# Conditioned adaLN block with memory attention on one core: a new prologue order, constants on VectorE, Wo and a memory update at other places, split last tiles

## The chip, the cores and the metric

The kernel runs on 1 core of one Trainium2 chip. A core has TensorE (PE, matrix products; its weight loads are listed as PEld), VectorE (DVE), ScalarE (ACT), GpSimd (POOL) and SyncE (SP). Here SP does nothing but issue DMAs; ACT issues some as well. Each engine works through its own instructions in order and waits for semaphores of the others. PE writes its products into PSUM, in buffers that DVE or ACT must read before they can be used again.

The metric is device time in microseconds (us) of one execution, as the median of several runs. Before the change it is 259.25 us (11 runs, 257.18 to 260.23).

## The reference

One transformer block on `x` of 2048 rows by 448, bf16, with 16 heads of 28. Cut to what matters:

```python
mod = (_silu(c) @ w_mod).reshape(c.shape[0], 6, 1, -1)          # six vectors of 448
sa, ca, ga, sb, cb, gb = ...
h = _layernorm(x) * (1 + ca) + sa
x = x + ga * _A_ref(h, A_wq, A_wk, A_wv, A_wo, A_beta)
h = _layernorm(x) * (1 + cb) + sb
x = x + gb * _B_ref(h, B_w_gate, B_w_up, B_w_down)

# _A_ref: 4 segments of 512 rows; per segment and head
p = _softmax(qs @ ks.T * scale + mask)          # causal inside the segment
a_dot = p @ vs
a_mem = (phi(qs) @ M) / (phi(qs) @ z + 1e-6)    # phi(t) = t + 1 if t > 0 else exp(t)
o = g * a_mem + (1 - g) * a_dot                 # g = sigmoid(beta)
M = M + phi(ks).T @ vs ;  z = z + sum(phi(ks))
# all heads together, then @ wo

# _B_ref: h = sigmoid(x @ w_gate) * (x @ w_up); h @ w_down      (448 -> 1792 -> 448)
```

## The kernel before, in words

The 2048 rows are four segments (`s`) of 512, each of four row tiles (`t`) of 128. The 448 columns are four chunks (`k` or `kc`), three of 128 and one of 64 (`LW`). The 16 heads are four groups (`hc`) of four. A pair (s, hc) is a unit of attention.

**An order written by hand.** The kernel is built under a manual schedule: the order in which Python emits instructions is their order on each engine. The main loop runs over `s`, `hc` and three logit groups `g` (0, 1, 2). In each step it emits the logits of the group (`logits`, L402), whose exponentials are ACT's, then for the unit before (`prev`) the memory read (`mem_read`, L457, at g = 0), the products with the values (`pv`, L429, at g = 1) and the transposing DMA of the result (`otr`, L482, at g = 2). The rest of PE's work is in a queue of jobs, `fill`, each with a cost in planned nanoseconds; `run_fill` (L584) takes as many as `pace` allows per step. Small work of DVE, POOL and SP is put off with `later(ns, ...)` (L76) until a planned clock, moved on by `tick` (L88), has passed; `need` (L92) forces what isn't due yet.

**Prologue (L639 to L679).** 18 products into an unused PSUM tile (`warm_up`). Norm of segment 0 (`LN`, L256). `mod_cols` (L212) makes columns of the modulation vectors by products with one moving column: (0, 0) gives `sa`, from `wm[0]`, which SP loads; (1, 1) gives `1 + ca`, from `wm[1]`, which ACT's queue loads; `mod_evac` (L230) copies them out of PSUM on DVE. 16 transposes on PE bring the normed tiles to column layout. `1 + ca` is folded into the rows of wq, wk (`pad_copy`, L618, on DVE, which also spreads heads from 28 to 32 columns) and wv (POOL, L673); `sa` becomes one more row of each (`bias_rows`, L627: products of a column of `sa` with wq, wk or wv; then a copy of the row into the weight). wq and wk first land in a staging part of `wd_sb`.

**Stages.** While the units of segment s are attended, `fill` works off the projections of later segments (`proj_qk` L335, `proj_v` L347), the memory updates (`mem_k` L373 makes phi of the keys and transposes it by DMA, `mem_update` L381 does the products `dM` and adds them to `M_sb`), and, from s = 1 on, what belongs to segment s - 1: four tiles of Wo (`wo_tile`, L492, with the second norm's statistics), gate and up (`gate_up` L514, `gate_up2` L533, a group of two chunks of 128 out of 14) and later down (`down`, L543, 14 products a tile, an add on DVE, the store). After the loop the last segment's Wo, gate, up and down follow.

**Queues and buffers.** All transposing DMAs (`pk`, `hT`, `oT`) and all stores of the output are issued by SP in the order of emission. PSUM has one tile `lg` of four banks for logits, and four buffers that everything else (pq, pv, acc, mem, dM, pwo, gps, ups, dps) shares in turn: the n-th allocation waits until the (n - 4)-th has been read. `acc` and `mem` are read by three DVE instructions, the last of which (L452 or L449, and L471) frees the buffer.

`KEEP` says how many gate and up groups a segment leaves for the next, `EARLY` is the first segment's pace, `NWARM` the number of warm-up products. `MM`, `MV`, `TR` and `GU` are the planner's costs of a product of 512 columns, of 448, of a transpose, and of a gate and up group.

Of the kernel before, what the change touches and what calls it, by code (L numbers as in the profile page):

```python
# [13 lines left out]
P = 128  # L14
# [3 lines left out]
def kernel(  # L18
# [34 lines left out]
    NWARM, EARLY, KEEP = 18, 2400.0, (0, 2, 2, 4)  # L53
# [111 lines left out]
    nc.gpsimd.memset(wo_sb[:], 0.0)  # L165
# [10 lines left out]
    for b in ou_bufs:  # L176
        nc.vector.memset(b[:, :, :, Dh:HP], 0.0)
    coef = const.tile([P, 2, H], F32)
# [10 lines left out]
    vt_all = [const.tile([P, TPS, H, ME + 1], BF16, name=f"vt{s}") for s in range(NSEG)]  # L189
    silu_bc = const.tile([KP, NK, P], BF16)  # L190

    def late_consts():
        nc.vector.tensor_copy(silu_bc[:], silu[:].rearrange("p (k o) -> p k o", o=1).to_broadcast([KP, NK, P]))
        for s in range(NSEG):
            nc.gpsimd.memset(vt_all[s][:, :, :, Dh:Dh + 1], 1.0)
# [5 lines left out]

        nc.gpsimd.memset(bmask[:], 1.0)
        for hs in range(4):
            nc.gpsimd.affine_select(out=bmask[:, :, hs, :], in_=bmask[:, :, hs, :], compare_op=ALU.is_ge,
                                    fill=0.0, base=-HP * hs, pattern=[[0, NHC], [0, ME]], channel_multiplier=1)
            nc.gpsimd.affine_select(out=bmask[:, :, hs, :], in_=bmask[:, :, hs, :], compare_op=ALU.is_ge,
                                    fill=0.0, base=HP * hs + Dh - 1, pattern=[[0, NHC], [0, ME]],
                                    channel_multiplier=-1)
# [220 lines left out]
    def pv(s, hc):  # L429
# [21 lines left out]
        t1 = work.tile([P, TPS * 4, Dh], F32, tag="t1", bufs=1)  # L451
# [5 lines left out]
    def mem_read(s, hc):  # L457
# [11 lines left out]
        t2 = work.tile([P, TPS * 4, Dh], F32, tag="t2", bufs=2)  # L469
# [21 lines left out]

    def wo_tile(s, t):  # L492
        need("wo")
        pw = m_f32("pwo")
        for k in range(NK):
            nc.tensor.matmul(pw[:, 0:D], lhsT=oT_of[s][:, k, t, :], rhs=wo_sb[:, k, :],  # L496
                             start=(k == 0), stop=(k == NK - 1))
# [7 lines left out]
        later(1500, lambda: ln.norm_t(t), ("ln2", s))  # L505
# [37 lines left out]
    def down(s, t):  # L543
        need("wd")
        dp = m_f32("dps")
        for fc in range(NFC):
            nc.tensor.matmul(dp[:, 0:D], lhsT=fT_of[(s, fc)][:, t * P:(t + 1) * P], rhs=wd_sb[:, fc, :],  # L547
                             start=(fc == 0), stop=(fc == NFC - 1))
        ot = work.tile([P, D], BF16, tag="ot", bufs=2)
        i = s * TPS + t  # L550
        nc.vector.tensor_tensor(ot[:], dp[:, 0:D], x_sb[:, i, :], ALU.add)  # L551
        nc.sync.dma_start(out_dram[i * P:(i + 1) * P, :], ot[:])


# [262 lines left out]
```

The softmax here doesn't subtract the row's maximum and nothing guards it: scores larger than these inputs give would overflow.

## Time and profile before

| | |
|---|---|
| median of 11 runs | 259.25 us (257.18 to 260.23) |
| the profiled execution: time | 259.45 us |
| its span, first to last instruction | 257.7 us |
| mean granted TensorE clock | 0.993 |
| HBM read, written | 10.67 MB, 1.84 MB |

The profile is of one execution. Its page counts, for each engine, the time in which it executes something; waiting, branches and the issuing of DMAs don't count. A line of the page names the code line, engine, operation and the tiles written and read; "idle before" is how long the engine had stood still, and what it stood for. The costliest groups:

```profile
L418 ACT ACTIVATE pT<-lg 128x2048 bf16<-128x2048 f32 (+1 forms) x48 | 76.8, 1599 | 27.3 <-PE lg L415 26.9
L426 POOL TENSOR_SCALAR_AFFINE_SELECT pT<-pT 128x512 bf16<-128x512 bf16 x64 | 42.8, 685 | 58.9 <-ACT pT L418 58.9
...
L541 DVE SCALAR_TENSOR_TENSOR fT<-tt,ups 128x512 bf16<-128x512 f32 x56 | 37.0, 685 | 32.9 <-PE ups L538 30.4
L547 PE MATMUL dps<-wd_sb,fT 128*128 128x448 bf16 x224 | 43.9, 352 | 0.0
L521 PE MATMUL gps<-hT,wg_sb 128*128 128x512 bf16 x154 | 40.3, 379 | 1.8 <-DVE t L452 1.0
```

After the bar stand the group's busy time and the mean length of one instruction in ns, then the idle time. Products on PE overlap: one of 512 columns is listed with some 380 ns, but they follow each other every 0.22 us in an undisturbed stretch. The chain of work that ended last, traced back from the end, is PE for 73% of the span and DVE for 13%.

### The profile page before, as it was taken

Reading aid. Unit: us, or ns where it says so; the run is one execution under the profiler, and the core shown is the slowest. Engines: PE = TensorE matmul, PEld = TensorE weight load, DVE = VectorE, ACT = ScalarE, POOL = GpSimd, SP = SyncE. Lnnn points to the kernel's source line nnn. Section 1 sums busy time; section 2 is a strip of 40 time slices with the busy share of each in tenths; the row PEclk is TensorE's granted clock in tenths of the full one; section 3 lists DMA queues with packets and bytes.
Section 4 is the critical chain, followed back from the end, with each engine's and each line's share of the span. In section 5 each row is a group of like instructions: output and inputs, shape, how many; then the busy total and the mean of one; then the engine's idle time right before and its main releaser. Section 6 shows DMA issues by size and latency. Waiting matters only on the chain.

```text
span 257.7 us, 5277 instructions
## 1 busy us (share of the span) xinstructions
PE 241.5 (94%) x2037; PEld 113.2 (44%) x2062; DVE 175.2 (68%) x412; ACT 139.1 (54%) x173; POOL 79.3 (31%) x146
## 2 busy tenths in 40 slices
PE   7799997999988899999999999999999999999994
PEld 2434533455544344544544534454344445333352
DVE  4878898577996768988965667886565485644411
ACT  1369878499859597876427767353653300133300
POOL 3388355141547221362602123352030023000000
PEclk9999999799999999999999999999999999999999
DMA  5999998577123103211221110123210013200011
GB/s 150 268 251 253 353 269 138 84 166 104 43 43 62 23 0 68 56 23 20 61 64 34 20 23 1 22 43 78 56 22 3 0 20 81 74 0 0 3 36 36
DMA packets 40992, 19.66 MB, mean 76 GB/s; under 512 B 29704, under 2 KB 40072, under 8 KB 40968
## 3 DMA queue, kind: packets, MB, share of 16 engines
q1 hardware_dynamic: 39544, 18.53, 32.1%
q10 hardware_dynamic: 1424, 0.80, 1.3%
q8 instruction: 16, 0.26, 0.5%
q14 instruction: 8, 0.07, 0.1%
HBM read 10.67 MB, written 1.84 MB: 49 GB/s over the span
## 4 chain that ended last, share of the span: by engine, by line
PE 73%; DVE 13%; DMA 5%; ACT 4%; issue 4%; POOL 1%; DVEq 0%; ACTq 0%
PE dps L547 17%; PE ups L538 12%; PE gps L521 12%; PE pq L340 8%; PE acc L440 5%; PE gps L526 5%; PE pwo L496 5%; PE lg L415 4%; DVE st L266 3%; DMA hT<-xn 2%; ACT pT L418 2%; DMA x_sb<-in_A_x_dram 2%; DVE xn L274 2%; PE pv L352 1%; PE dM L388 1%
## 5 line engine op out<-in xcount | busy, mean ns | idle before, releaser
L418 ACT ACTIVATE pT<-lg 128x2048 bf16<-128x2048 f32 (+1 forms) x48 | 76.8, 1599 | 27.3 <-PE lg L415 26.9
L426 POOL TENSOR_SCALAR_AFFINE_SELECT pT<-pT 128x512 bf16<-128x512 bf16 x64 | 42.8, 685 | 58.9 <-ACT pT L418 58.9
L529 ACT ACTIVATE tt<-gps 128x512 f32<-128x512 f32 x56 | 30.4, 596 | 56.1 <-PE gps L526 56.1
L541 DVE SCALAR_TENSOR_TENSOR fT<-tt,ups 128x512 bf16<-128x512 f32 x56 | 37.0, 685 | 32.9 <-PE ups L538 30.4
L547 PE MATMUL dps<-wd_sb,fT 128*128 128x448 bf16 x224 | 43.9, 352 | 0.0
L521 PE MATMUL gps<-hT,wg_sb 128*128 128x512 bf16 x154 | 40.3, 379 | 1.8 <-DVE t L452 1.0
L538 PE MATMUL ups<-hT,wu_sb 128*128 128x512 bf16 x165 | 40.6, 381 | 0.3 <-issue 0.2
L547 PEld LDWEIGHTS <-fT 128*128 128x128 bf16 x224 | 21.5, 98 | 19.9 <-issue 0.2
L270 POOL TENSOR_SCALAR rs<-mv 128x1 f32<-128x1 f32 (+2 forms) x21 | 5.9, 283 | 61.4 <-DVE mv L267 58.6
L521 PEld LDWEIGHTS <-wg_sb 128*128 128x128 bf16 x168 | 15.8, 98 | 19.6 <-DVE t L452 1.6
L538 PEld LDWEIGHTS <-wu_sb 128*128 128x128 bf16 x168 | 14.1, 97 | 20.9 <-issue 6.8
L266 DVE BATCH_NORM_STATS2 st<-x_sb 128x6 f32<-128x448 bf16 x32 | 19.8, 619 | 2.5 <-DMA x_sb<-in_A_x_dram 2.0
L440 PE MATMUL acc<-vt,pT 128*128 128x29 bf16 x640 | 18.7, 175 | 1.5 <-DVE t L471 1.0
L440 PEld LDWEIGHTS <-pT 128*128 128x128 bf16 x640 | 17.6, 96 | 4.8 <-issue 2.1
L340 PE MATMUL pq<-hT,wq_sb 128*128 128x512 bf16 x58 | 16.4, 381 | 2.5 <-DMA hT<-xn 2.3
L340 PE MATMUL pq<-hT,wk_sb 128*128 128x512 bf16 x62 | 17.4, 396 | 1.2 <-DVE t L452 1.1
L551 DVE TENSOR_TENSOR ot<-dps,x_sb 128x448 bf16<-128x448 f32 x16 | 9.9, 621 | 12.5 <-PE dps L547 9.4
L526 PE MATMUL ups<-hT,wgu_sb 64*128 64x512 bf16 x56 | 17.7, 382 | 0.5 <-DVE t L452 0.5
L415 PE MATMUL lg<-qT,kT 28*128 28x512 bf16 (+3 forms) x256 | 17.5, 305 | 0.5 <-ACT pT L418 0.5
L274 DVE TENSOR_SCALAR xn<-x_sb,mv,rs 128x448 bf16<-128x448 bf16 x32 | 14.1, 457 | 5.6 <-POOL rs L271 5.6
L526 PE MATMUL gps<-hT,wgu_sb 64*128 64x512 bf16 x56 | 16.9, 381 | 0.1
L271 POOL TENSOR_TENSOR rs<-rs,mhalf 128x1 f32<-128x1 f32 (+2 forms) x21 | 13.8, 656 | 1.8
(101 smaller groups left out, 262.1 us busy)
## 6 DMA issues: line engine op xcount, KB each, us to landing
wm<-in_w_mod_dram SPq DMA_DIRECT2D x5, 392.0 KB, 6.3
out_dram<-ot SPq DMA_DIRECT2D x16, 112.0 KB, 1.7
x_sb<-in_A_x_dram SPq DMA_DIRECT2D x3, 448.0 KB, 4.7
wd_sb<-in_B_w_down_dram SPq DMA_DIRECT2D x3, 448.0 KB, 9.9
wg_sb<-in_B_w_gate_dram SPq DMA_DIRECT2D x3, 448.0 KB, 9.8
wu_sb<-in_B_w_up_dram SPq DMA_DIRECT2D x3, 448.0 KB, 10.2
wm<-in_w_mod_dram ACTq DMA_DIRECT2D x1, 392.0 KB
wo_sb<-in_A_wo_dram SPq DMA_DIRECT2D x4, 98.0 KB
```

What stands on the lines that cost most here:

```text
L266: nc.vector.bn_stats(st[:], self.srcs[i])
L340: nc.tensor.matmul(pq[:, 0:L], lhsT=head_cols(w_sb, k, hc), rhs=h[:, k, :], start=(k == 0), stop=(k == NK - 1))
L415: nc.tensor.matmul(lg[:, hs, wid:wid + nq], lhsT=kT[r, hc, kb * P:(kb + 1) * P], rhs=qT[r, hc, kb * P:L], start=True, stop=True, tile_posi ...
L418: nc.scalar.activation(pT[:, :, w0:w0 + wid], lg[:, :, 0:wid], AF.Exp, scale=scale)
L426: nc.gpsimd.affine_select(out=blk, in_=blk, compare_op=ALU.is_ge, fill=0.0, base=0, pattern=[[0, 4], [1, P]], channel_multiplier=-1)
L440: nc.tensor.matmul(accv[:, qb, hs, 0:ME], lhsT=pT[:, hs, c0:c0 + P], rhs=vt[:, kb, hc * 4 + hs, 0:ME], start=(kb == 0), stop=(kb == qb))
L521: nc.tensor.matmul(g[:, 0:L], lhsT=wg_sb[:, k, f], rhs=h[:, k, :], start=(k == 0), stop=False)
L526: nc.tensor.matmul(dst[:, 0:L], lhsT=wgu_sb[r:r + LW, f], rhs=h[r:r + LW, 3, :], start=first, stop=not first, tile_position=(r, 0))
L529: nc.scalar.activation(tt[:], g[:, 0:L], AF.Tanh, scale=0.5)
L538: nc.tensor.matmul(u[:, 0:L], lhsT=wu_sb[:, k, f], rhs=h[:, k, :], start=False, stop=(k == 2))
L541: nc.vector.scalar_tensor_tensor(ft[:], tt[:], 1.0, u[:, 0:L], op0=ALU.add, op1=ALU.mult)
L547: nc.tensor.matmul(dp[:, 0:D], lhsT=fT_of[(s, fc)][:, t * P:(t + 1) * P], rhs=wd_sb[:, fc, :], start=(fc == 0), stop=(fc == NFC - 1))
```

## The change

- **Prologue.** `NWARM` is 20, and a product without use stands after each group of four transposes and after the bias rows. `mod_cols(((1, 1),))` comes first, `mod_cols(((0, 0),))` after half of the transposes; `mod_evac` and the norms change places to suit. The bias rows of wq and wk are made together, that of wv later and alone; the first two projections follow each other.
- **Constants.** The fills of `wo_sb`, of `bmask` and of the ones in `vt` go from POOL to DVE, to the start; the eight selects that shape `bmask` stay on POOL, and go to the start too.
- **Segment 2's norm** (`ln1_start(2)`) is started ahead of segment 1's transposes.
- **Wo one group sooner.** The jobs of segment s - 1 are put into `fill` at (hc 0, g 2) instead of (hc 1, g 0), with jobs of the old tail between the Wo tiles in another pattern; there the transposing DMA `otr` is emitted ahead of the fill work. The second norm's scaling is put off by 2400 planned ns instead of 1500, but for the last segment.
- **The third memory update** (`m[2]`) goes from the loop of s = 1 to that of s = 2.
- **t1 and t2**, the attention's two summands, become bf16.
- **The end.** `KEEP` is 3 for the last segment, the pace there divides by 10; a number of jobs (`run_jobs`) replaces planned time around the last unit; the first two Wo tiles do their first three chunks ahead of the last chunk's wait. Stores of segments 2 and 3 go out by ACT's queue. The last tile of all is done in two halves of 224 columns.

```diff
-    NWARM, EARLY, KEEP = 18, 2400.0, (0, 2, 2, 4)
+    NWARM, EARLY, KEEP = 20, 2400.0, (0, 2, 2, 3)
...
-    nc.gpsimd.memset(wo_sb[:], 0.0)
...
+    nc.vector.memset(bmask[:], 1.0)
+    for hs in range(4):
+        nc.gpsimd.affine_select(out=bmask[:, :, hs, :], ...)
+        nc.gpsimd.affine_select(out=bmask[:, :, hs, :], ...)
+    nc.vector.memset(wo_sb[:], 0.0)
+    for vt in vt_all:
+        nc.vector.memset(vt[:, :, :, Dh:Dh + 1], 1.0)
...
     def late_consts():
-        for s in range(NSEG):
-            nc.gpsimd.memset(vt_all[s][:, :, :, Dh:Dh + 1], 1.0)
...
-        nc.gpsimd.memset(bmask[:], 1.0)
-        for hs in range(4):
-            nc.gpsimd.affine_select(...)
...
-        t1 = work.tile([P, TPS * 4, Dh], F32, tag="t1", bufs=1)
+        t1 = work.tile([P, TPS * 4, Dh], BF16, tag="t1", bufs=1)
...
-        t2 = work.tile([P, TPS * 4, Dh], F32, tag="t2", bufs=2)
+        t2 = work.tile([P, TPS * 4, Dh], BF16, tag="t2", bufs=2)
...
+    def wo_mm(s, t, ks):
+        need("wo")
+        if t not in pw_of:
+            pw_of[t] = m_f32("pwo")
+        for k in ks:
+            nc.tensor.matmul(pw_of[t][:, 0:D], lhsT=oT_of[s][:, k, t, :], rhs=wo_sb[:, k, :],
+                             start=(k == 0), stop=(k == NK - 1))
     def wo_tile(s, t):
+        wo_mm(s, t, range(NK))
+        wo_fin(s, t)
...
-        later(1500, lambda: ln.norm_t(t), ("ln2", s))
+        later(1500 if s == NSEG - 1 else 2400, lambda: ln.norm_t(t), ("ln2", s))
...
     def down(s, t):
...
+        eng = nc.scalar if s >= NSEG - 2 else nc.sync
+        n = 2 if i == NSEG * TPS - 1 else 1
+        for h in range(n):
+            c = slice(h * D // n, (h + 1) * D // n)
+            for fc in range(NFC):
+                nc.tensor.matmul(dp[:, c], lhsT=fT_of[(s, fc)][:, t * P:(t + 1) * P], rhs=wd_sb[:, fc, c], ...)
+            nc.vector.tensor_tensor(ot[:, c], dp[:, c], x_sb[:, i, c], ALU.add)
+            eng.dma_start(out_dram[i * P:(i + 1) * P, c], ot[:, c])
...
-        return [(0, lambda: [later(2000 * hc, ...
+        return [(0, lambda: [later((2000 if s < 2 else 1500) * hc, ...
...
+    def run_jobs(n):
+        for _ in range(n):
+            cst, fn = fill.popleft()
+            fn()
+            tick(cst)
...
-    mod_cols(((0, 0),), warm[:, 1, :])
-    for t in range(TPS):
+    mod_cols(((1, 1),), warm[:, 2, :])
+    for t in range(2):
         ln0.norm(t)
-    mod_evac(((0, 0),))
+    mod_evac(((1, 1),))
+    for t in range(2, TPS):
+        ln0.norm(t)
     pts = [m_bf16("lntr") for _ in range(NK)]
-    for t in range(TPS):
+    def ln0_tr(t):
         for kc in range(NK):
             nc.tensor.transpose(pts[kc][:, t * P:(t + 1) * P], ln0.xn[:, t, kc * P:(kc + 1) * P], ident[:])
-    mod_cols(((1, 1),), warm[:, 2, :])
+        warm_up(1)
+    ln0_tr(0)
+    ln0_tr(1)
+    mod_cols(((0, 0),), warm[:, 1, :])
+    mod_evac(((0, 0),))
+    for k in range(2):
+        pad_copy(nc.vector, wq_sb, wq_st, k)
+    ln0_tr(2)
+    ln0_tr(3)
     for kc in range(NK):
         ln0.pe_evac(pts[kc], kc, True)
-    mod_evac(((1, 1),))
-    evac_q, = bias_rows((wq_st,))
-    for k in range(NK):
-        pad_copy(nc.vector, wq_sb, wq_st, k)
+        if kc == 1:
+            pad_copy(nc.vector, wq_sb, wq_st, 2)
+    evac_q, evac_k = bias_rows((wq_st, wk_st))
+    pad_copy(nc.vector, wq_sb, wq_st, 3)
+    warm_up(1)
     evac_q(nc.scalar.copy, wq_sb[LW:LW + 1, 3, :, 0:Dh])
     for k in range(NK):
         pad_copy(nc.vector, wk_sb, wk_st, k)
+    evac_k(nc.vector.tensor_copy, wk_sb[LW:LW + 1, 3, :, 0:Dh])
...
     j0[0][1]()
-    evac_k, evac_v = bias_rows((wk_st, wv_sb))
-    evac_k(nc.vector.tensor_copy, wk_sb[LW:LW + 1, 3, :, 0:Dh])
+    j0[1][1]()
+    evac_v, = bias_rows((wv_sb,))
...
-    ... + j0[11:] + ln1_pe_jobs(1) + [ln1_start(2)] + j1[:4] ...
+    ... + j0[11:] + [ln1_start(2)] + ln1_pe_jobs(1) + j1[:4] ...
...
+                if prev[0] >= 0 and g == 2 and hc == 0:
+                    otr(*prev)
-                if s >= 1 and hc == 1 and g == 0:
+                if s >= 1 and hc == 0 and g == 2:
...
-                    for w in wo_jobs(s - 1):
+                    for t, w in enumerate(wo_jobs(s - 1)):
+                        n = 2 if s > 1 or t == 0 else t % 2
+                        fill.extend(tail[:n])
+                        tail = tail[n:]
                         fill.append(w)
-                        if tail and s > 1:
-                            fill.extend(tail[:2])
-                            tail = tail[2:]
...
                         dj = down_jobs(s - 2)
+                        if s == 2:
+                            gj = m[2][0:1] + gj[:6] + m[2][1:] + gj[6:]
...
-                        fill.extend(h2_jobs(s - 1) + gj[:2] + m[2][0:1] + gj[2:10] + m[2][1:] + gj[10:])
-                    pace[0] = (cost(fill) - KEEP[s] * GU) / (12 if s < 3 else 9)
+                        fill.extend(h2_jobs(s - 1) + gj)
+                    pace[0] = (cost(fill) - KEEP[s] * GU) / (12 if s < 3 else 10)
...
-                if prev[0] >= 0 and g == 2:
+                if g == 2 and hc > 0:
                     otr(*prev)
...
-    run_fill(2000)
+    run_jobs(4)
     pv(last, NHC - 1)
     tick(1100)
-    run_fill(1500)
+    run_jobs(1)
     otr(last, NHC - 1)
-    run_fill(3500)
-    for c, fn in wo_jobs(last):
-        fn()
-        tick(c)
-    fill.extend(dj)
+    run_jobs(1)
+    for t in range(2):
+        wo_mm(last, t, range(NK - 1))
+    tick(6 * MV)
+    for t in range(TPS):
+        wo_mm(last, t, range(NK - 1 if t < 2 else 0, NK))
+        wo_fin(last, t)
+        tick((200, 1400, 760, 760)[t])
+    fill.extendleft(reversed(dj))
```

## The prediction

> **What bounds the kernel now.** First the page's busy shares and the granted clock, then the engine windows, then the list of what TensorE waited for, then the timeline around the largest waits, last DMA landings.
>
> ```profile
> PE 241.5 (94%) x2037; PEld 113.2 (44%) x2062; DVE 175.2 (68%) x412; ACT 139.1 (54%) x173; POOL 79.3 (31%) x146
> ...
> PEclk9999999799999999999999999999999999999999
> ```
>
> TensorE (PE) is busy 94% of 257.7 us and the change takes no product away, so a gain must come from the other 16 us or from clock. Of those, 1.4 us lie before the first instruction of PE and about 3.3 us behind its last (the last down product starts at 254.06). The clock row has one dent, the 7 in its eighth slice (45 to 51.5 us).
>
> ```profile
> 43.50:45.60 2.10, 0.00 (x0) 0.00 (x0) 2.03 (x6) 1.19 (x2) 2.05 (x4) 1.00 0.50 70
> 46.40:49.90 3.50, 3.50 (x20) 1.48 (x19) 1.75 (x3) 1.30 (x2) 0.00 (x0) 0.51 0.63 80
> ```
>
> Windows, with PE first and the granted clock third from the end: PE stands still for 2.1 us, and 0.8 us later its clock is 0.51 for 3.5 us. That idle time is paid twice: its own length, and 3.5 x 0.49 = 1.7 us.
>
> ```profile
> PE pq L340 <- DMA hT<-xn: 2.3, 1, 2.3
> ...
> PE pq L340 <- DVE t L452: 1.1, 1, 1.1
> PE acc L440 <- DVE t L471: 1.0, 1, 1.0
> PE gps L521 <- DVE t L452: 1.0, 1, 1.0
> PE warm L225 <- DVE silu L187: 0.9, 1, 0.9
> PE pv L352 <- DVE kT L345: 0.6, 1, 0.6
> PE ups L526 <- DVE t L452: 0.5, 1, 0.5
> ```
>
> Waits of PE (total, times, longest). The first is that still-stand: segment 2's first projection waits for its transposed activations. L452, L471 and L345 are VectorE (DVE) instructions that free a PSUM buffer: DVE, far from busy on average, is 7.3 to 7.6 of 8 us busy at 32 to 40 and 64 to 80 us, and late there.
>
> **The prologue: a loss.** `mod_cols(((1, 1),))` now stands ahead of `mod_cols(((0, 0),))` and of every transpose in PE's order. It reads wm1, loaded on ACT's queue.
>
> ```profile
> 1.80 0.49 ACTq L117 DMA_DIRECT2D wm<-in_w_mod_dram  x1
> ...
> 9.84 0.47 SPq L137 DMA_DIRECT2D wv_sb<-in_A_wv_dram  x1
> ...
> 10.29 0.54 PE L225 MATMUL warm<-silu,wm 112*128 112x1 bf16 x16
> ```
>
> The loads of wm land 6.3 to 9.8 us after issue, median 8.0; SP's L137 waited 2.1 us for a wm load and went out at 9.84, which with 1.80 + 8.0 = 9.8 puts wm1's landing there. Before, PE came to it at 10.29 and did not notice. Now PE ends 20 fillers at 7.4 + 2 x 0.22 = 7.8 and stands until 9.85. Then: wm1's 16 columns end at 10.4 (0.54); `cols` on DVE at 10.7, and norms 2 and 3 queue behind it to 11.4 (2 x 0.36; before 10.0). Two transposed tiles with fillers 4 x 0.23 to 11.3, wm0's columns to 11.85, two more tiles and fillers to 12.75. DVE meanwhile: sa_bf 12.2, two wq pads 12.7 (0.27 each), hT 13.1, pad 13.4, hT 13.75, pad 14.0, four wk pads 15.1 (1.07), wk's bias row 15.75 (0.62). The key projection closes at 16.0 (before 15.1). The bias row of wv, four products that shared kv slots before, now stands alone behind it (0.19 each by the starts of L632: 0.8), then the second query projection (0.9): first logits at 17.7 against 16.08, **+1.6**. Bounds: 0, if wm1 flew like wm0 (issued at 1.31, PE's wait for it over at 7.40: 6.1 us, so landing at 7.9), and +1.6; I take the latter, being the landing seen. Five more fillers inside this stretch lie in DVE's shadow and cost nothing of their own; 0.22 each if they did not.
>
> The moved constants hide: DVE idles 2.0 us before the first L266 at 5.08, and the added memsets come to 0.25 + 0.9 + 4 x 0.1 = 1.55 (by the 256-word 0.27 and 128-word 0.17). GpSimd (POOL) gets eight mask selects of 0.33, from 3.5 to 6.2, ahead of its rs at 6.75. Cover gone, each delays the norms one for one. POOL's scaling of wv (5.56 us, L673) starts behind wv's bias row, now at 16.2 instead of 13.6, and ends at 21.8; the first value projection, 21.17 before, comes at 22.8: 1.0 of slack, beyond which PE waits.
>
> **20 to 46 us: a gain.**
>
> ```profile
> 21.55 1.23 POOL L195 MEMSET vt<- 128x64 bf16 x4
> 21.57 1.62 DVE L197 TENSOR_SCALAR coef<-coef 128x16 f32<-128x16 f32 x1 [1.11 <-ACT coef L196]
> ...
> 22.35 0.80 POOL L202 MEMSET bmask<- 128x464 bf16 x1
> ...
> 23.22 0.17 DVE L198 TENSOR_SCALAR coef<-coef 128x16 f32<-128x16 f32 x1
> ```
>
> A 16-column DVE operation takes 1.62 us, as long as POOL's memsets beside it; the like-sized L198 takes 0.17. The memsets leave, so 1.45 comes back. The norms of segment 1 then end at about 26.2 (before 26.0, now with the prologue's +1.6 inside), but PE, later too, no longer waits for them: transposes 26.5 to 27.4 instead of 24.9 to 26.75, and the first projection closes at 28.5 against 28.0. So 1.1 of the 1.6 is recovered.
>
> Segment 2's stats now start one group earlier; from the last hT copy to its last norm DVE has 10.7 us of work (five L266/L267 pairs of 0.77, three kT of 0.68, three phi of 0.75, one ou of 1.1, four norms of 0.37) instead of 12.3 (seven pairs), so that norm ends at 39.0, not 40.15. On SP two of its four transposes (1.2 us issue each) go out ahead of the third pk instead of behind. The last is issued at 40.5, not 41.66, and lands 3.1 later at 43.6. PE arrives at 43.2 to 43.7 (before 43.24; +0.5, less some of the 0.6 at L345). Projection starts at 43.7 against 45.67: **-2.0**, the prologue's loss included. Bounds: -3.3 (no loss there) and +1.6 (no recovery). With 0.5 us or less idle the clock should stay: **-1.7**, between -1.75 and 0.
>
> The Trainium skill ("TensorE: Matmul & The Clock Gate", Why this matters for your kernels) asks only that PE not idle longer than about 3 us between bursts; here 2.1 to 2.4 us sufficed, so the trace decides. The same page (Part 4) says transposes do not count as activity for the clock. That speaks against the new prologue, which from 7.8 to 12.7 holds little but transposes and one-column products; by that rule I should add another 1.7 there, while the row shows 1.00 from 8.4 to 11.2 through the like work.
>
> **70 to 98 us: a gain.** From the memory read of unit (1,0) to the key projection that needs `acc`'s buffer, PE has 6.5 us of work (3 Wo tiles, logits, acc, Wo, dM, pq). DVE has 1.1 + 6.5 = 7.6, hence the wait of 1.1. Wo is queued one group sooner, behind two jobs of the old tail, and the transpose of the last unit goes out on SP ahead of that fill work, so oT is there no later. The new order puts dM after the first Wo tile, delays the norms (2400 planner ns for 1500) and puts the unit's t1 ahead of the third Wo tile: 1.1 + 5.9 = 7.0, wait 0.5. Next, `acc` of (1,1) waited 1.0 for L471; in the new allocation order it takes a buffer that ScalarE frees. Third, L521 waited 1.0 for an L452 queued behind L288, which stood for a DMA; t1 now precedes L288. Fourth, 0.5 at L526: segment 2's `phi` work is gone from here. Of 3.6 I take **-2.6**; bounds -3.6 and 0.
>
> The third memory update reappears in the next segment: DVE 4 x 0.7 + 0.63 = 3.4 us, ScalarE 4 x 0.63, dM 0.84 on PE unchanged, four pk transposes on SP of 1.2 each ahead of the next oT. Windows there show DVE at 4.9 to 7.4 of 8. Nothing to +3.4; with all other new waits I take **+1.0**. bf16 t1/t2: L452 and L471 read PSUM at 0.62 still; L453 gains at most 0.3, off PE's path except at the end.
>
> **200 us to the end.** Before, the last `acc` stood 0.5 for ScalarE (L529) since all four buffers were out; it now follows the up half. From its end the chain to the last oT is 1.1 + 0.3 to 0.6 + 2.45 DMA = 4.2 us; PE's cover is one gate/up group (3.2, from L521 to L521 in the last stage) + six Wo products 1.1 = 4.3. The stalls of 0.5 (L440) and 0.5 (L496) go: **-1.0**, 0 if DVE is late again. Out stores of the last two segments leave SP, so segment 3's last transpose is not behind a store (SP 217.30, then 217.92): PE's stutter at 220.8 to 221.7, **-0.4**, bounds 0 and -0.6. ScalarE then waits for `ot`, with its tanh queued behind; it idles 16.6 us there, so nothing. The halved last tile: DVE 0.62 to about 0.34, **-0.3**; bounds -0.5 (some of the store's 1.7 to landing too) and +0.5 (a second issue on ScalarE's queue, 0.5 by its L117). The Trainium skill ("DMA: Bandwidth & Descriptors", Specifications) names 512 B as the least for line rate, and the halved rows are 448 B; no run here prices it.
>
> **Sum** on the profiled execution (259.45, span 257.7, so 1.75 around it): -2.0 -1.7 -2.6 +1.0 -1.0 -0.4 -0.3 = -7.0; span 250.7, time **252.5**. The median of 11 runs is 259.25, 0.2 below the profiled one; they spread from 257.18 to 260.23.
>
> **Rivals.** (a) Slower: wm1's wait sets off the clock. PE idles 2.0 us from 7.8, much as at 43.5; half clock follows over the projections (+1.7), hT of segment 2 moves with everything (+1.6), PE still idles there and the second dent stays, and DVE's waits merely shift: 259.45 + 3.3 = 262.7. It decides if idle before segment 2 remains at 2 us or more. For it: the single dent followed such an idle; against: DVE's shortened list. (b) DVE remains the limit at 70 to 98 (it was 7.35 of 8 busy): -2.6 becomes 0, 255.1. (c) wm1 lands by 8.4: another 1 to 1.6 off, and the waits at their better bounds, 250. (d) The fillers and moves only exchange waits: 259.
>
> **Chances.** Forecast 0.45, (c) 0.17, (b) 0.20, (d) 0.08, (a) 0.10. About 0.5% (1.3 us) is what a measurement of this kernel can tell from no change. Faster: 0.45 + 0.17 + 0.20 = 0.82; same 0.08; slower 0.10. The range runs from 249.5 (all but the best of (c)) to 256.5 (b with 1.4 of further waits), leaving (a) and (d) out.
>
> **What would show it.** In the new profile: PE's L225 waiting some 2 us for a wm load, first L415 near 17.7; no DVE operation of 1.6 us on `coef`; under 1 us at the first L340 of segment 2 and no dent in the clock row behind it; L452 and L471 gone from the top waits; no 0.5 at the last L440. I am wrong if wm1 is there in time, if the dent stays, or if segment 2 shows new waits above 1 us each.

## The result and the profile after

The change makes the kernel slower: 261.14 us (12 runs, 259.93 to 261.9) against 258.83 us (46 runs, 257.18 to 260.29), a ratio of 1.009 with a 95% interval of 1.0065 to 1.0116. The forecast was 252.5, range 249.5 to 256.5. The profiled execution after took 260.25 us with a span of 258.5, before 259.45 and 257.7.

Two rows of the page after, busy share of TensorE and granted clock by slice:

```profile
PE 241.0 (93%) x2057; PEld 114.8 (44%) x2083; DVE 173.1 (67%) x419; ACT 139.5 (54%) x173; POOL 75.7 (29%) x140
PEclk9999999999999999999999999999999999999999
```

PE's busy time hardly moved (241.5 before), and this execution has no half-clock slice. The waits of PE after (total, times, longest):

```profile
PE warm L225 <- DMA wm<-in_w_mod_dram: 1.6, 1, 1.6
...
PE gps L531 <- DVE hT L288: 1.3, 1, 1.3
PE pq L340 <- DVE ou L449: 1.2, 1, 1.2
PE ups L536 <- DVE t L452: 1.1, 1, 1.1
...
PE dM L388 <- DMA pk<-e: 0.8, 1, 0.8
PE pv L352 <- DVE t L471: 0.7, 1, 0.7
PE ups L536 <- DVE t L471: 0.6, 1, 0.6
PE gps L531 <- DVE t L452: 0.6, 1, 0.6
...
PE dps L563 <- DVE ot L565: 0.5, 1, 0.5
```

Gone are the 2.3 us for hT at segment 2's first projection, the 1.1 and the 1.0 at a projection and an `acc` in the loop of s = 1 (75 and 81.5 us), the 0.5 at the last `acc` and the 0.9 at the first columns. New are the wait for wm1, a wait of the same first projection for another operation (L449), a group at L531/L536 and dM, and one inside the split tile. Where they stand shows when the two profiles are laid side by side by the starts of the same exponential (L418) of each unit, after minus before ("this stretch" is the growth since the row above; that of the second row counts from the start, as its forecast does):

| stretch, up to | difference there | this stretch | forecast |
|---|---|---|---|
| first logits | +2.0 | | (+1.6) |
| segment 2's first projection, 45.69 against 45.67 us | 0.0 | 0.0 | -2.0 |
| (0, 3, 1), behind the half-clock window of before | -1.5 | -1.5 | -1.7 |
| (2, 0, 0), 98.6 us | -2.9 | -1.4 | -2.6 |
| (3, 0, 2), 155.6 us | +2.1 | +5.0 | +1.0 |
| end of the span | +0.8 | -1.3 | -1.7 |

So 5.0 us are lost in the loop of s = 2, and the start of the forecast's gains, segment 2's projection, did not move at all. What VectorE did in the worst stretch, first before the change, then after it (timeline: start, length, what; in brackets its idle time before and for what):

```profile
126.00 0.29 DVE L366 TENSOR_SCALAR r<-qT 128x512 bf16<-128x512 bf16 x1
...
128.72 0.61 DVE L453 TENSOR_TENSOR ou<-t,t 128x448 bf16<-128x448 f32 x1
130.28 1.38 DVE L288 TENSOR_SCALAR hT<-hT,cols 128x512 bf16<-128x512 bf16 x4 [0.94 <-issue]
```

```profile
121.84 1.19 DVE L274 TENSOR_SCALAR xn<-x_sb,mv,rs 128x448 bf16<-128x448 bf16 x2
...
123.98 0.61 DVE L565 TENSOR_TENSOR ot<-dps,x_sb 128x448 bf16<-128x448 f32 x1
128.94 0.74 DVE L288 TENSOR_SCALAR hT<-hT,cols 128x512 bf16<-128x512 bf16 x2 [4.35 <-DMA hT<-xn]
129.59 0.29 DVE L366 TENSOR_SCALAR r<-qT 128x512 bf16<-128x512 bf16 x1
129.99 0.43 DVE L367 TENSOR_TENSOR e<-e,r 128x512 bf16<-128x512 bf16 x1
```

Before, the phi of the next memory read (L366) and a unit's sums (up to L453) stood ahead of the scaling of hT (L288). Now VectorE stands 4.35 us at that scaling, whose last row tile was normed at 123, and behind it wait the phi and the two units' `t`, which free PE's buffers. PE's timeline after:

```profile
130.47 0.39 PE L464 MATMUL mem<-rm,e 128*128 128x116 bf16 x4 [0.34 <-DVE e L367]
131.50 0.81 PE L531 MATMUL gps<-hT,wg_sb 128*128 128x512 bf16 x2 [0.64 <-DVE t L452]
132.67 0.81 PE L531 MATMUL gps<-hT,wg_sb 128*128 128x512 bf16 x3 [0.37 <-DVE ot L565]
...
134.68 0.39 PE L536 MATMUL ups<-hT,wgu_sb 64*128 64x512 bf16 x1 [0.64 <-DVE t L471]
...
140.69 0.39 PE L536 MATMUL ups<-hT,wgu_sb 64*128 64x512 bf16 x1 [1.06 <-DVE t L452]
...
147.87 0.38 PE L388 MATMUL dM<-vt,pk 128*128 128x116 bf16 x4 [0.77 <-DMA pk<-e]
```

The listed lengths of products overlap, so a bracket is some 0.17 us less than what PE lost by the starts (one product of 512 columns follows another in 0.22 us). By the starts PE lost 0.51, 0.81, 0.53 and 0.81 between 129.7 and 134.7, then 1.22 at 139 and 0.93 at 147 round the moved memory update: 4.8 of the 5.0 us. Before there were no waits above 0.5 between 97 and 200 us. Below, a wait of PE in a fence is the profile's, one in the text mostly counted by the starts.

A reading aid for the experiments: of 93 runs of the kernel before that stood beside them, 34 had the full clock (median 257.66) and 59 mostly one half-clock window of 3.4 us (259.39), after the change 5 of 12 (260.25) and 7 (261.36), so it is slower in both groups.

### The profile page after: what moved, and what is told of

Same layout as the page of the kernel before. It is cut to its first block, busy times and chain, and to the rows that moved or that the text cites. A ratio compares the mean times of both kernels' runs of the same rounds, so it can differ in the third digit from the quotient of the medians.

```text
span 258.5 us, 5310 instructions
## 1 busy us (share of the span) xinstructions
PE 241.0 (93%) x2057; PEld 114.8 (44%) x2083; DVE 173.1 (67%) x419; ACT 139.5 (54%) x173; POOL 75.7 (29%) x140
## 4 chain that ended last, share of the span: by engine, by line
PE 56%; DVE 5%; DMA 3%; ACT 3%; issue 2%; POOL 1%; SPq 0%; DVEq 0%
PE dps L563 14%; PE gps L531 13%; PE ups L548 13%; PE gps L536 5%; PE pwo L499 4%; PE acc L440 3%; PE lg L415 3%; DMA hT<-xn 2%; ACT pT L418 2%; DMA pk<-e 1%; PE mem L464 1%; ACT tt L539 1%; DVE e L367 1%; DVE ot L565 1%; POOL pT L426 1%
## 5 line engine op out<-in xcount | busy, mean ns | idle before, releaser
L418 ACT ACTIVATE pT<-lg 128x2048 bf16<-128x2048 f32 (+1 forms) x48 | 76.7, 1598 | 28.3 <-PE lg L415 28.1
L551 DVE SCALAR_TENSOR_TENSOR fT<-tt,ups 128x512 bf16<-128x512 f32 x56 | 37.2, 687 | 40.9 <-PE ups L548 36.5
L563 PE MATMUL dps<-wd_sb,fT 128*128 128x448 bf16 (+1 forms) x238 | 44.1, 342 | 0.5 <-DVE ot L565 0.5
L531 PE MATMUL gps<-hT,wg_sb 128*128 128x512 bf16 x156 | 40.1, 379 | 3.1 <-DVE hT L288 1.3
L563 PEld LDWEIGHTS <-fT 128*128 128x128 bf16 x238 | 22.8, 98 | 19.2 <-issue 0.6
L531 PEld LDWEIGHTS <-wg_sb 128*128 128x128 bf16 x168 | 15.6, 98 | 20.3 <-issue 2.0
L440 PEld LDWEIGHTS <-pT 128*128 128x128 bf16 x640 | 17.5, 96 | 3.3 <-issue 1.5
L536 PE MATMUL ups<-hT,wgu_sb 64*128 64x512 bf16 x56 | 17.4, 382 | 1.7 <-DVE t L452 1.1
L440 PE MATMUL acc<-vt,pT 128*128 128x29 bf16 x640 | 18.6, 175 | 0.0
L270 POOL TENSOR_SCALAR rs<-mv 128x1 f32<-128x1 f32 (+2 forms) x21 | 5.4, 256 | 43.9 <-DVE mv L267 40.9
L536 PE MATMUL gps<-hT,wgu_sb 64*128 64x512 bf16 x56 | 16.9, 381 | 0.2
L565 DVE TENSOR_TENSOR ot<-dps,x_sb 128x448 bf16<-128x448 f32 (+1 forms) x17 | 10.1, 593 | 10.0 <-PE dps L563 10.0
L340 PE MATMUL pq<-hT,wk_sb 128*128 128x512 bf16 x62 | 16.4, 380 | 0.2
L352 PE MATMUL pv<-wv_sb,hT 128*128 128x448 bf16 x64 | 13.4, 353 | 1.3 <-DVE t L471 0.7
```

Source lines behind the costliest of these rows:

```text
L340: nc.tensor.matmul(pq[:, 0:L], lhsT=head_cols(w_sb, k, hc), rhs=h[:, k, :], start=(k == 0), stop=(k == NK - 1))
L418: nc.scalar.activation(pT[:, :, w0:w0 + wid], lg[:, :, 0:wid], AF.Exp, scale=scale)
L440: nc.tensor.matmul(accv[:, qb, hs, 0:ME], lhsT=pT[:, hs, c0:c0 + P], rhs=vt[:, kb, hc * 4 + hs, 0:ME], start=(kb == 0), stop=(kb == qb))
L531: nc.tensor.matmul(g[:, 0:L], lhsT=wg_sb[:, k, f], rhs=h[:, k, :], start=(k == 0), stop=False)
L536: nc.tensor.matmul(dst[:, 0:L], lhsT=wgu_sb[r:r + LW, f], rhs=h[r:r + LW, 3, :], start=first, stop=not first, tile_position=(r, 0))
L551: nc.vector.scalar_tensor_tensor(ft[:], tt[:], 1.0, u[:, 0:L], op0=ALU.add, op1=ALU.mult)
```

## The experiments

The kernel before stood beside each group of runs, with medians from 258.71 to 259.20 us. So medians of different groups (below) can differ by some 0.5 us for no reason of the kernel's; the ratio is the safer column.

| run | kernel run | median, us | ratio to the kernel before (95% interval) |
|---|---|---|---|
| x1_wm1_first | after, wm1 loaded first | 261.72 | 1.0079 (1.0047 to 1.0111) |
| x8_wu_late_wm1 | x1, wu loaded late | 259.49 | 1.0029 (1.0001 to 1.0057) |
| y2_prologue_back | after, old prologue | 261.31 | 1.0065 (1.0022 to 1.0108) |
| w1_before_wu_late | before, wu loaded late | 259.02 | 1.0006 (0.9978 to 1.0035) |
| x2_mem3_back | after, memory update back | 262.82 | 1.0133 (1.0085 to 1.018) |
| x4_delay1500 | after, norm delay 1500 | 264.38 | 1.0209 (1.0168 to 1.0249) |
| z1_wo_s2_back | after, Wo of s = 2 back | 260.59 | 1.0077 (1.0048 to 1.0107) |
| x6_mod_later | after, L288 later | 259.18 | 0.9999 (0.9963 to 1.0036) |
| y1_wo_back | after, old main loop | 257.58 | 0.9951 (0.9921 to 0.9981) |
| x3_stores_act | after, all stores on ACT | 264.22 | 1.0167 (1.0115 to 1.022) |
| y3_end_back | after, old end | 264.47 | 1.0216 (1.0168 to 1.0264) |
| x5_unsplit | after, last tile whole | 260.55 | 1.0066 (1.0036 to 1.0096) |
| z3_combined | old loop, loads moved, tile whole | 254.69 | 0.9829 (0.9797 to 0.986) |
| w2_moved_timed | new loop with all repairs | 256.53 | 0.991 (0.9873 to 0.9947) |
| w3_old_prologue | z3 with old prologue | 255.23 | 0.9859 (0.9824 to 0.9894) |
| w4_two_buffers | z3, split in two buffers | 254.42 | 0.9839 (0.9801 to 0.9877) |

### The prologue and segment 2's projection

```diff
-    wm = {0: load_wm(nc.sync, 0), 1: load_wm(nc.scalar, 1)}
+    wm = {1: load_wm(nc.sync, 1), 0: load_wm(nc.scalar, 0)}
```

> The changed kernel with the queues of the first two modulation loads exchanged: wm1 by SP, wm0 by ACT's queue; the order of every engine is as it was. Theory (the loss is the prologue's wait of 1.6 us for wm1 plus some 5 us of new waits in segment 2): the wait at L225 falls from 1.6 us to under 0.4, the first logits come at 16.2 to 16.8 us instead of 18.05, and most of it lasts to the end: 259.0 to 260.0 us against 261.1. Rival 'the prologue does not matter, a later wait takes it all': the first logits move, the time stays within 0.5 us of 261.1. Rival 'the prologue is the whole loss': 258 or less.

A miss, and a useful one. PE's wait at L225 fell to 0.5 us and the first logits (from here on by the first exponential's start, 18.64 in the change) came at 17.15 us, 1.5 sooner, but the projection of segment 2 started at 45.55 us, with 2.7 us of idle PE in front, and the time is no better. Three profiles (before, after, x1), with first logits up to 2 us apart, all start it at 45.55 to 45.69; profiles of other runs with the changed prologue start it between 45.56 (x4) and 47.32 (y3). The DMA share points to the reason. A window of the change, then of x1 (length, then busy time of PE, PEld, DVE, ACT, POOL, the clock, the DMA share and GB/s; a transfer is counted where it starts, so a share can exceed 1):

```profile
36.00:40.00 4.00, 4.00 (x30) 1.60 (x27) 3.74 (x11) 3.05 (x4) 0.77 (x1) 1.00 1.28 191
36.00:40.00 4.00, 3.74 (x60) 2.19 (x59) 3.79 (x12) 3.95 (x5) 0.21 (x1) 1.00 1.35 216
```

The sixteen DMA engines are still full at 36 to 40 us, with 4.8 MB of wd, wg and wu issued from 16 to 30 us. So wu, first used at 84 us, was moved out of the way:

```diff
-        + ... + [piece(wu_sb, B_w_up, k) for k in range(NK)]
...
-    fill.extend(j2[:2] + m[0][1:] + j2[2:3] + ...)
+    fill.extend(j2[:2] + m[0][1:] + sp(lambda: [piece(wu_sb, B_w_up, k)() for k in range(NK)]) + j2[2:3] + ...)
```

> The changed kernel with wm1 loaded first (as in the run of that name) and, in addition, the four loads of wu (1.6 MB, first used at 84 us) issued at some 54 us instead of 26 to 30 us; PE's order is as it was. Theory formed from the first runs: the projection of segment 2 starts at 45.67 to 45.69 us before, after the change and with wm1 first, however early VectorE's norms are, because its hT transposes queue behind the weight loads that keep the DMA engines full from 16 to 39 us. Then the fourth hT goes out by 41 us, the projection starts at 44.3 us or sooner (VectorE's ou at 44.06 is next), PE idles 1.5 us or less there instead of 2.74, and the time falls by 1.2 to 2 us against wm1 first: 259.7 to 260.5. Rival 'the order on SP and VectorE sets it': start stays at 45.7, time at 261.7 within 0.5.

Confirmed. SP's queue after the change, then in x8 (start, length of the issue):

```profile
35.79 3.87 SPq L284 DMA_TRANSPOSE hT<-xn  x2
39.76 1.22 SPq L377 DMA_TRANSPOSE pk<-e  x1
41.07 2.52 SPq L284 DMA_TRANSPOSE hT<-xn  x2
```

```profile
34.44 2.52 SPq L284 DMA_TRANSPOSE hT<-xn  x2
37.05 1.22 SPq L377 DMA_TRANSPOSE pk<-e  x1
38.35 2.52 SPq L284 DMA_TRANSPOSE hT<-xn  x2
```

And the window of x8 to lay beside that of x1:

```profile
36.00:40.00 4.00, 3.88 (x64) 2.31 (x61) 3.79 (x12) 3.82 (x5) 0.07 (x1) 1.00 0.51 104
```

With the DMA share down to 0.51 the first pair goes out in 2.5 us instead of 3.9, the last hT leaves SP at 40.9 instead of 43.6, and the projection starts at 44.3. What it waits for now is what the waits after already named, `ou` L449: it frees the PSUM buffer, and stands on VectorE behind three norms of segment 3.

For y2 the prologue's and the constants' lines of the change's diff were put back.

> The changed kernel with the prologue and the constants as before the change (18 fillers, wm0's columns first, constants on GpSimd); segment 2's norms still start sooner, and the main loop and the end stay changed. Theory (what the prologue loses is swallowed by the wait for segment 2's hT, which is set by the DMA engines): first logits at 16.7, projection of segment 2 at 45.7 all the same, 261.1 within 0.7 us. Rival 'the prologue's 2 us last to the end': 259.5 or less.

As expected in the time: the whole old prologue gives first logits at 16.6 us, 2.0 sooner, and 261.31 us. The projection of segment 2 starts at 46.57 in its profile, not at 45.7, with a gap of 3.1 us in front and a half-clock window behind; the profiled execution took 262.23 us, in runs from 258.2 to 264.62, so this shows only that the 2.0 us were not kept.

The same move of wu in the kernel before:

> The kernel before the change, with wu's four loads issued behind segment 3's hT transposes (some 54 us) instead of at 26 to 30 us, and nothing else. Theory (in the kernel before, too, segment 2's projection waited for weight traffic, not for VectorE's norms as the forecast had it): the wait for hT falls from 2.3 us to under 1.2, the projection starts at 43.7 to 44.7 instead of 45.67, the half-clock window behind it becomes rare: 257.0 to 258.0 us against 258.9. Rival 'the norms set it': start at 45.2 or later, time within 0.5 us of the kernel before.

Half a miss. In the kernel before, the wait for hT falls only from 2.3 to 1.5 us (start 44.8): there all four transposes stand behind the third pk and leave SP one after the other from 38.1 to 43.3, so the order counts as well as the traffic. The time did not fall at all, as the rival had it: the last oT of segment 0 leaves SP at 65.13 as before (65.08), and PE, now 2.0 us ahead, waits 1.2 us for it at L496.

### The main loop

```diff
-                            gj = m[2][0:1] + gj[:6] + m[2][1:] + gj[6:]
+                            gj = gj[:6] + [(16 * TR, lambda: None)] + gj[6:]
...
-                        fill.extend(h2_jobs(s - 1) + gj)
+                        fill.extend(h2_jobs(s - 1) + gj[:2] + m[2][0:1] + gj[2:10] + m[2][1:] + gj[10:])
```

> The changed kernel with the third memory update back in the loop of s = 1 (its planned cost is left as an empty job in s = 2, so that the pace there stays). Theory (in segment 2 VectorE stands at L288 for a late hT, and the memory update adds only the waits at 139 and 147 us): those two, 1.2 and 0.9 us, go, the wait of 4.35 us at L288 stays above 3, and 70 to 98 us get 1 us longer: 259.5 to 261 us. Rival 'the moved memory update makes the loss of segment 2': L288's wait falls below 1.5 us as well and the time to 256.5 to 258.

Here `mem_jobs` has its old delay too. The waits at 139 and 147 us went, but the four from 129 to 134 went as well. What is left of PE's waits from 120 to 150 us, and VectorE's hold-up:

```profile
PE lg L415 <- ACT pT L418: 0.3, 1, 0.3
132.63 0.76 DVE L288 TENSOR_SCALAR hT<-hT,cols 128x512 bf16<-128x512 bf16 x2 [2.53 <-DMA hT<-xn]
```

L288 still stands 2.53 us ahead of the phi, more than the rival's 1.5, but PE has down tiles to do meanwhile and comes to the next memory read only at 139.84. So for the waits of segment 2 the rival is borne out. But the time rose. With the memory update back in s = 1, the sooner Wo finds VectorE full there:

```profile
PE acc L440 <- DVE t L471: 1.5, 1, 1.5
PE lg L415 <- ACT pT L418: 0.8, 1, 0.8
PE gps L531 <- DVE hT L288: 0.8, 1, 0.8
```

These waits of PE from 68 to 98 us are followed by the clock: windows of x2, the clock third from the end.

```profile
82.70:89.50 6.80, 5.77 (x18) 1.31 (x18) 3.60 (x10) 2.42 (x5) 0.92 (x2) 0.50 0.35 33
```

Two half-clock windows, 3.4 us. Laid beside the change's profile, x2 loses 4.4 us between (0, 3, 1) and (2, 0, 0), and a new wait of 1.1 us stands at 185 us. So the moved memory update is in the loss of segment 2, but given the sooner Wo it is better moved.

```diff
-        later(1500 if s == NSEG - 1 else 2400, lambda: ln.norm_t(t), ("ln2", s))
+        later(1500, lambda: ln.norm_t(t), ("ln2", s))
```

> The changed kernel with the second norm put off by 1500 planned ns in every segment, as before the change, instead of 2400. Theory (the four Wo tiles fall on VectorE in one bunch from 114 to 121 us and the delayed norms queue behind them): the first xn of segment 1's second norm comes 1 to 2 us sooner than 119.3, the last by 0.5 to 1; L288's wait shrinks by 0.5 to 1.2 us: 260.0 to 260.7. Rival 'the delay is the cause': wait under 1.5 us, 258.5 or less. Rival 'no part of it' (norms follow the bunch either way): 261.1 within 0.3.

All three readings missed: 264.38. In segment 2 the wait only shrank to 3.4 us, but from 69 to 81 us three norms, now called sooner, stand waiting for POOL's `rs` (0.48, 0.75 and 0.99 us of idle VectorE), PE waits behind them, and the clock was 0.57 from 81 to 89 us. The delay of 2400, which the forecast named only within the 0.6 us that it took off the first wait at 70 to 98 us, is worth some 3 us here.

```diff
-                if s >= 1 and hc == 0 and g == 2:
+                if s >= 1 and (hc, g) == ((1, 0) if s == 2 else (0, 2)):
...
+                        if s == 2:
+                            fill.append(w)
                         fill.extend(tail[:n])
                         tail = tail[n:]
-                        fill.append(w)
+                        if s != 2:
+                            fill.append(w)
```

> The changed kernel with the Wo jobs of segment 1 alone put in at (hc 1, g 0) again, in the old pattern (a Wo tile, then two jobs of the old tail), that is in the loop of s = 2; in s = 1 and s = 3 they stay one group sooner, and the third memory update stays in segment 2. Theory (in segment 2 the two old-tail groups go out ahead of the Wo tiles, these then fall together, VectorE works their adds and statistics off in one bunch, and the hT transposes come late against the down tiles that cover them): L288's wait falls from 4.35 us to under 1.5 us, the waits of PE from 129 to 134 us (2.7 us) go, those at 139 and 147 us (2.1 us) stay: 258 to 259.3 us. Rival 'the memory update in segment 2 is what delays VectorE': 260.5 us or more.

My theory fell: with Wo's tiles of s = 2 back at their old place and pattern, L288 still waited 4.7 us and PE's four waits stayed; only the one at 147 us went. It is not the bunch of Wo tiles. The time, 260.59, is the rival's, and x2 had already shown the four waits to go with the memory update. What remained of the theory was the queue behind L288:

```diff
-                later(6500 + 400 * kc, lambda kc=kc: ln.modulate(kc, 2), ("ln2", s))
+                later((6500 if s != 1 else 9500) + 400 * kc, lambda kc=kc: ln.modulate(kc, 2), ("ln2", s))
```

> The changed kernel with segment 1's second scaling (L288) put off by 9500 planned ns instead of 6500, so that phi, the memory read's and the unit's operations stand ahead of it on VectorE; PE's order and SP's are as they were. Theory (VectorE's queue behind L288 is what PE waits for, more than hT itself): of PE's 2.7 us of waits from 129 to 134 us at most 1.5 remain, and the time falls by 0.8 to 1.5 us: 259.6 to 260.4. Rival 'hT's lateness alone counts, the queue behind it not': within 0.4 us of 261.1.

Confirmed, and larger than expected. PE's order and the transposes are the same. VectorE's timeline:

```profile
125.75 0.28 DVE L366 TENSOR_SCALAR r<-qT 128x512 bf16<-128x512 bf16 x1
126.14 0.43 DVE L367 TENSOR_TENSOR e<-e,r 128x512 bf16<-128x512 bf16 x1
...
128.64 0.38 DVE L453 TENSOR_TENSOR ou<-t,t 128x448 bf16<-128x448 bf16 x1
129.73 1.44 DVE L288 TENSOR_SCALAR hT<-hT,cols 128x512 bf16<-128x512 bf16 x4 [0.71 <-DMA hT<-xn]
```

hT lands as late as ever, but its 4.35 us of waiting are filled with the phi and the unit's sums, and of PE's waits from 120 to 150 us two are left, both at the memory update:

```profile
PE dM L388 <- DMA pk<-e: 0.8, 1, 0.8
PE ups L536 <- DVE t L452: 0.7, 1, 0.7
```

Between (2, 2, 2) and (2, 3, 2) this takes 2.8 us out, the sum of the four waits (2.7). So with the update left where the change put it, L288's place alone decides them.

For y1 the loop's lines of the change's diff, the delays of the norms and of `mem_jobs`, and the pace divisor of 9 were put back.

> The changed kernel with the main loop as before the change: Wo's jobs put in at (hc 1, g 0) between the old tail's jobs in the old pattern, otr behind the fill work, norms put off by 1500, the third memory update in the loop of s = 1. Prologue, constants, bf16 and the end stay changed. Theory (the moved Wo and memory update lose 3.2 us net between 66 and 190 us): 257.3 to 258.7 us, and L288 in segment 2 waits less than 1.5 us. Rival 'prologue and end lose it': 260.5 or more.

Confirmed in the time, 257.58. L288 stands idle for 2.0 us there, more than the 1.5 expected, but with nothing behind it that PE needs: from 97 to 200 us the profile has one wait of PE, 0.2 us.

### The end

```diff
-        eng = nc.scalar if s >= NSEG - 2 else nc.sync
+        eng = nc.scalar
```

> The changed kernel with all output stores on ACT's queue, so that none stands between the transposes of hT on SP. Theory: the third hT transpose goes out at 123.5 instead of 124.3 us; L288's wait falls by 0.6 to 0.8 us, of which the end gets 0.4 to 0.8: 260.3 to 260.7. Rival 'SP's order is what makes hT late': the wait at L288 falls by 2 us or more, 259 or less. Rival 'ScalarE then waits for ot with the exponentials behind it': slower, 262 or more.

The third reading was right. ScalarE's waits from 120 to 138 us: two exponentials stood 6.2 us behind a store that waited for its `ot`.

```profile
ACT pT L418 <- DVE ou L453: 6.2, 1, 6.2
ACT pT L418 <- POOL xn L278: 6.2, 1, 6.2
```

The releasers named are chance; the issue of the store, on the same engine, stands just in front of each. In the change only stores behind the last exponential use ACT's queue, so there it cost nothing.

```diff
-    run_jobs(4)
+    run_fill(2000)
...
-    run_jobs(1)
+    run_fill(1500)
...
-    for t in range(2):
-        wo_mm(last, t, range(NK - 1))
...
-    fill.extendleft(reversed(dj))
+    run_fill(3500)
+    for c, fn in wo_jobs(last):
+        fn()
+        tick(c)
+    fill.extend(dj)
```

> The changed kernel with the end as before the change: KEEP 4 and planned time instead of counted jobs behind the loop, Wo's last tiles whole, the last down tile in one piece (the pace divisor of 10 and the stores on ACT's queue stay). Theory (the new order of the end is worth 1.0 us at the last acc and Wo tile, the split tile costs 0.4): 261.3 to 262.1. Rival 'the end is where it loses': 260.3 or less.

A miss: behind the changed loop the new end is worth 3.3 us by the medians. In the profile, (3, 3, 2) to the last product takes 3.0 us longer with the old end: waits of 0.5 for ScalarE at L440 and at L499, 0.5 for VectorE at L499 and 0.9 at the down tiles. That is not what the change gained by it: in the kernel before, the old end had just the waits of 0.5 (L440) and 0.3 (L496), and from (3, 3, 2) to the end of the span the change is 0.9 us shorter.

```diff
-        n = 2 if i == NSEG * TPS - 1 else 1
+        n = 1
```

> The changed kernel with the last down tile in one piece. Theory (both halves lie in one PSUM tile and the second half's products wait 0.65 us for VectorE's read of the first; that costs more than the shorter last add saves): last tile's end 0.3 to 0.5 us sooner, 260.6 to 260.9 us. Rival 'the halves save what I forecast': 261.4.

Confirmed in the profile: from the third tile's add to the end of the last, 3.71 us split and 3.27 whole.

```profile
252.21 0.62 DVE L565 TENSOR_TENSOR ot<-dps,x_sb 128x448 bf16<-128x448 f32 x1 [2.02 <-PE dps L563]
253.55 0.39 DVE L565 TENSOR_TENSOR ot<-dps,x_sb 128x224 bf16<-128x224 f32 x1 [0.72 <-PE dps L563]
255.53 0.39 DVE L565 TENSOR_TENSOR ot<-dps,x_sb 128x224 bf16<-128x224 f32 x1 [1.59 <-PE dps L563]
```

These are the adds after the change: the second half comes 1.98 us after the first, though its 14 half-wide products take 1.34. They wait for the first half's add, since both halves are one PSUM tile. With a tile for each half (`dp = m_f32("dps")` inside the loop over `h`, on top of z3_combined):

> As z3_combined, but with the last tile split as in the change, each half in a PSUM tile of its own. Theory (what made the split lose was the shared tile: the products of the second half waited 0.5 us for the read of the first): no wait of PE at L563, the last add 0.39 instead of 0.62 us: 0.1 to 0.3 us sooner than z3, 254.4 to 254.6. Rival 'the second store or the half-wide products cost as much': 254.7 or more.

```profile
248.32 0.39 DVE L565 TENSOR_TENSOR ot<-dps,x_sb 128x224 bf16<-128x224 f32 x1 [0.72 <-PE dps L563]
249.66 0.39 DVE L565 TENSOR_TENSOR ot<-dps,x_sb 128x224 bf16<-128x224 f32 x1 [0.95 <-PE dps L563]
```

1.34 us apart, and from the third tile's add to the end 3.07 us instead of 3.27: 0.2 of the 0.3 us that the change looked for. The medians (254.42 and 254.69) and the ratios (0.9839 and 0.9829) do not tell the two kernels apart.

### Put together

The pieces that helped, in one kernel: y1's loop, x8's loads, x5's whole tile.

> Main loop as before the change (as in y1_wo_back), with wm1 loaded first, wu's loads late (as in x8_wu_late_wm1) and the last tile in one piece; constants, bf16, segment 2's earlier norms and the new end stay. Theory: the gains add, since they lie in different stretches: 257.6 - 1.0 to 1.6 - 0.4 = 255.6 to 256.3. Rival 'what the prologue brings is given back at 70 to 98 us, where VectorE and the hT transposes set the pace': 257 to 257.6.

Better than the sum: 254.69 us, all six runs between 254.58 and 254.86 and none with a half-clock window. Part of what adds up is therefore likely clock: of the two idle stretches that set it off elsewhere, the one at 8 us is gone in its profile and the one at 43 us is down to 1.4.

The new loop with x8's loads, x6's delay and x5's whole tile:

> The changed kernel with all repairs found but with its moved main loop kept: wm1 first, wu's loads late, segment 1's scaling put off by 9500, last tile in one piece. Theory (the gains add: 261.1 - 1.6 - 2.0 - 0.4; the waits at 138 and 145 us for the moved memory update stay): 256.7 to 257.5, so the moved loop stays 2 us or more behind the old one at the same repairs (254.7). Rival 'with L288 placed late the moved loop is as good': 255.2 or less.

Confirmed, slightly better: the moved loop, with L288 placed late, is 1.8 us behind the old loop at the same repairs. Its profile keeps the waits of 0.8 for pk at dM and of 0.4 for `t` beside it, and one of 1.6 at 82 us for L288 in segment 1's loop.

And z3 with the old prologue and constants, wm0 first:

> As z3_combined (old main loop, wu late, last tile whole, new end), but with prologue and constants as before the change and wm0 loaded first. Theory (with wm1 there in time the new prologue still brings its first logits 0.4 us later than the old one, and takes 0.9 us back at segment 1's norms, where the old one has a 1.6 us operation on coef): 254.7 to 255.4. Rival 'the new prologue loses at any order of the loads': 254.2 or less.

Confirmed: the old prologue's first logits are 0.4 us sooner (16.72 against 17.15), and from (0, 1, 1) on it is 0.76 behind. With wm1 there in time the new prologue is worth 0.5 us.

## Why the prediction was wrong

The profiled execution missed the forecast by 7.8 us: 4.0 of them in the loop of s = 2, 2.0 at segment 2's projection, 1.2 at 70 to 98 us, 0.6 in the rest.

- **The prologue** went as worked out: PE stood for wm1 (1.6 us at L225), `cols` held norms 2 and 3, first logits 2.0 us later for 1.6. The constants hid, and 0.9 of it came back at segment 1's norms where the 1.6 us operation on `coef` had been (+1.97 to +1.09).
- **"Lands 3.1 later at 43.6 ... Projection starts at 43.7 against 45.67: -2.0"** failed. Its first half held: the last norm ended at 38.98 (forecast 39.0) and the transposes went out in the order named. But the last was issued at 42.4 instead of 40.5, for the larger part since weight traffic filled the DMA engines until 39 us (x8: from the last norm to the last issue 2.0 us instead of 3.4). It took the row's 1.2 us per issue from an undisturbed stretch. And it did not follow what else that projection needs: L449, behind segment 3's norms, ends at 45.63, so even a prompt hT would have gained nothing in this profile. The Trainium skill ("Trainium Kernel Development and Optimization", Key Constraints) says that DMAs of all queues share the same 16 engines and interleave; the share of 1.28 beside a 3.9 us pair, and 0.51 beside a 2.5 us pair, agree with it.
- **The clock, -1.7**: it came in the profiled pair (1.5) but was a property of that execution. A third of the runs of before have no such window, and 7 of 12 after have one. Against the median it could have been worth some 1.1 (59 of 93 x 1.7).
- **70 to 98 us, -2.6**: right in place, -1.4 in size. The waits for L452 at the projection and at L440 went as said, but a new one for L471 came at the value projection (0.7), and the third, for an L452 behind L288, became one of 1.3 for L288 itself, at which VectorE stands 1.5 us for hT.
- **"Nothing to +3.4; with all other new waits I take +1.0"** is the step that decided: it was +5.0. The forecast counted VectorE's added work (3.4) and judged it by the mean load of the stretch. The runs show VectorE's order instead. 2.8 us come from L288, which, placed by planned time, now reaches the head before hT has landed and blocks the phi and sums that PE needs (x6). The rest, 2.1 us of waits at 139 and 147, stands round the moved memory update. These are no two separate prices: with the update back (x2) all six waits go, with L288 later (x6) the four. The four need both. "Where a stall goes, what is late next" was not asked for L288. z1 refuted my first explanation, Wo's bunching, and x4 the second, the delay alone. x2 shows that the moved update shifts PE's work against L288; why the planned place slipped against hT in just this combination was not taken apart further.
- **200 us to the end**: -1.3 for -1.7. The waits at L440 and at the Wo tile went as said. The halves were given -0.3 and cost +0.44: the wait inside the tile was not among the bounds' reasons. The halved rows themselves cost nothing that showed: the two half stores landed in 1.6 us, the whole ones on the same queue in 1.7.
- **Rivals**: (d), waits only exchanged, with 259 comes nearest to the profiled 260.25, (a), the slower case, with 262.7 to the median of 261.14. Of (a) one part is real: in four profiles (x2, y3, z1, x6) the wait for wm1 lasted 2.6 to 2.9 us and half clock followed from 11.0 or 12.0 us; where it lasted up to 2.0 it did not. The rest of (a) did not decide: 1.2 us of the idle time before segment 2 remained, less than the 2 it named, and the loss lay behind it.

## What to carry to other kernels

A gain in front of a wait is worth only what that wait leaves, so before costing it, list everything the waiting instruction needs, with the DMA share of the stretch and the order on the engine that frees its buffer. An operation that waits for a DMA on an in-order engine is priced by what is queued behind it, and moving a producer means placing its consumer anew. Edits of an order written by hand are coupled: of the parts of the moved loop, three put back one at a time (Wo's place for s = 2 alone) gave 260.6 to 264.4 us, and all together 257.6.

## What the runs showed of the hardware

The half clock comes in whole windows of 3.41 us (two of them from 82.7 in x2), and the same kernel shows it in some executions only. The length of the idle time alone does not decide it: by the profile, single waits of PE of 2.3 us (before, until 45.67), 1.6 us (x3, until 127.16) and 1.5 us (x2, until 81.07) were followed by half clock within 2 us, one of 2.6 us (x1, until 45.55) was not. The Trainium skill ("TensorE: Matmul & The Clock Gate", Why this matters for your kernels) asks for no idle gap above some 3 us; here gaps of half that length were followed by half clock too.
